# A two-layer transformer stack on one core: 72 of the second attention's exponentials computed on VectorE, and idle matmuls placed on open sums

## The chip, the cores and the metric

The kernel runs on one core of a Trainium2 chip. The engines that matter are TensorE (PE, with its weight loads shown as PEld), ScalarE (ACT), VectorE (DVE) and the DMA queue of SyncE (SP). The metric is the device time of one launch in microseconds (us); of several timed runs the median counts. A profiled execution gives the trace; its time stands beside its span below.

## The reference, cut to what matters

Four blocks run one after the other on `x` (2048 rows of 1024, bf16): linear attention A, softmax attention B, then A and B again with the same weights. "First" and "second attention" below are the two runs of B. There are 32 heads of 32 columns.

```python
def _B_ref(x, wqkv, wo):
    qkv = (x @ wqkv).reshape(B, S, 3, H, Dh).transpose(2, 0, 3, 1, 4)
    q, k, v = qkv[0], qkv[1], qkv[2]
    scores = einsum("bhqd,bhkd->bhqk", q, k) * (Dh ** -0.5)
    p = softmax(scores, axis=-1)
    o = einsum("bhqk,bhkd->bhqd", p, v)
    return o.transpose(0, 2, 1, 3).reshape(B, S, D) @ wo

x = x + A(layernorm(x));  x = x + B(layernorm(x))
x = x + A(layernorm(x));  x = x + B(layernorm(x))
```

One attention makes 32 x 2048 x 2048 exponentials.

## The kernel before, in words

**Order.** Nothing is issued directly. Every piece of work is an `Op` with an engine, a planned duration, dependencies, buffers and a priority. `Sched.run` plays the program with these planned durations and writes down the order in which each engine would start its pieces; the instructions are then emitted in that order, and each engine works its own list strictly in order. Buffers come from an arena in SBUF and from the eight PSUM banks, with a quota for each class (`QUOTA`).

**Attention** (`attention`, L893 on). The work falls into 32 turns, one for each pair of a chunk of 512 queries (`qc`) and a group of four heads (`g`): first chunks 0 and 1 for all groups (turns 0 to 15), then chunk 2 (16 to 23) and chunk 3 (24 to 31). A turn has 64 units. A unit is the 128 x 512 scores of one head: 128 keys against 512 queries. Units are taken three at a time (`WIDE`): three score matmuls (L922), which lie on different 32-row strips of the PE array, fill three PSUM banks, and one ACTIVATE of 128 x 1536 (L928) writes their exponentials to SBUF as bf16. Two such sets of three banks alternate (banks 0 to 5). Per attention that is 682 ACTIVATEs of 1536 columns and one of 1024.

The exponentials are then multiplied with the values and with ones (L956), four matmuls on four 32-column strips at a time, and summed in bank 6 over the whole of half a turn. VectorE copies the sum out of bank 6 (L968); two DMAs on SP move the denominators, VectorE takes four reciprocals (L979) and multiplies (L983).

**Filler.** Bank 7 serves everything else that runs during an attention: the projections of keys (`b_k`), queries (`b_q`, `q_away`) and values (`b_v`), and the output projection, all through L401 as four column strips and each copied out by VectorE (L814, L822, L838). The queries are multiplied by 1/sqrt(32) on that way.

**Idle matmuls.** If PE finds nothing to start in the planned time while scores are live, and has worked less than `KEEP` = 75% of the last `SPELL` = 3.4 planned us, `Sched.run` puts one matmul with no use (`idle`, onesD times x) into bank 7, provided bank 7 is free and no filler holds it. In the trace these are the `xT,onesD` matmuls of L401.

**Pointer operand.** Of all ACTIVATEs before the change, those at L477 alone (the logarithm in the layer norm) take their bias from a 128 x 1 tile, `eps`; the others, L928 too, have scale and bias as constants in the instruction.

Of the kernel before, what the change touches and what calls it, by code (L numbers as in the profile page):

```python
# [2 lines left out]

# [8 lines left out]
AX = mybir.AxisListType  # L12
BF16 = mybir.dt.bfloat16
F32 = mybir.dt.float32

EPS_LN = 1e-5
EPS_DEN = 1e-6
DH = 32
# [12 lines left out]


class Op:
    __slots__ = ("eng", "dur", "lat", "fn", "bufs", "prio", "mode", "ndep", "out", "t", "start", "seq")

    def __init__(self, eng, dur, lat, fn, bufs, prio, mode, seq):
        self.eng, self.dur, self.lat, self.fn, self.bufs = eng, dur, lat, fn, bufs
        self.prio, self.mode, self.seq = prio, mode, seq
        self.ndep, self.out, self.t, self.start = 0, [], 0.0, None


LAT = {"PE": 0.25, "ACT": 0.2, "DVE": 0.1, "POOL": 0.2, "SP": 2.0, "AQ": 2.0}
# [3 lines left out]
class Sched:  # L46
    def __init__(self, sbuf_bytes, quota):
        self.ops = []
        self.quota = quota
        self.live = {}  # L50
        self.free = [(0, sbuf_bytes)]
        self.bank_used = [False] * 8
        self.peak = 0
        self.total = sbuf_bytes
        self.queue = {}
        self.idle = None
# [86 lines left out]
    def run(self):  # L143
# [16 lines left out]
        todo = sorted(o.prio for o in self.ops)  # L160
        front = 0
        recent = []
        started = {}
        for o in self.ops:
            if o.ndep == 0:
# [2 lines left out]
        while left:  # L168
            moved = False
            for e in engines:  # L170
                if busy[e] > t + 1e-9 or not ready[e]:
                    continue
                skipped = []
                pick = None
                while ready[e] and len(skipped) < 60:
                    item = heapq.heappop(ready[e])
                    if item[0] <= todo[front] + WINDOW and self._alloc(item[2].bufs):
                        pick = item[2]
                        break
                    skipped.append(item)  # L180
                for s in skipped:
                    heapq.heappush(ready[e], s)
                if pick is None and e == "PE" and self.idle is not None and self.live.get("S", 0):

                    recent = [r for r in recent if r[1] > t - SPELL]
                    worked = sum(r[1] - max(r[0], t - SPELL) for r in recent)
                    if worked < KEEP * SPELL and not self.live.get("fil", 0) and not self.bank_used[7]:
                        pick = Op("PE", MM, LAT["PE"], self.idle, (Buf("ps", 0, "idle", [(7,)]),), 0.0, "c", 0)
                        pick.bufs[0].left = 1
                        self.queue["idle"] = [list(pick.bufs), 0]  # L190
                        assert self._alloc(pick.bufs)
                        left += 1
                if pick is None:
                    continue
                if e == "PE":
                    recent.append((t, t + pick.dur))
                d = pick.dur
                if pick.mode is not None:
                    if mode[e] is not None and mode[e] != pick.mode:
                        d += SWITCH  # L200
                    mode[e] = pick.mode
                pick.start = t
                if pick.fn is not self.idle:
# [12 lines left out]
            if moved:  # L216
                continue
            if not events:
                stuck = [(o.prio, o.eng, [(b.cls, b.at) for b in o.bufs]) for e in engines for _, _, o in ready[e]][:8]
                raise AssertionError(f"nothing can start at {t:.1f}: {left} left, {stuck}, live {self.live}")  # L220
            t = events[0][0]
            while events and events[0][0] <= t + 1e-9:
                _, _, o, own = heapq.heappop(events)
                if not own:
                    for b in o.bufs:
                        b.left -= 1
                        if b.left == 0:
# [17 lines left out]
QUOTA = {"pk": 3, "pv": 2, "kv": 1, "ln": 2, "mm": 2, "cmp": 2, "bc": 4, "num": 1, "wt": 4, "fil": 2,  # L245
         "e": 6, "vp": 6, "e1": 4, "vp1": 4, "E": 5, "q2": 3, "kt": 3, "w2": 8, "w2o": 3, "oT": 26, "T": 4, "den": 2,
         "lnt": 6, "lnw": 2, "lnw1": 1, "eq": 8, "ns": 4, "cw": 6, "hl": 6, "oc": 2, "slab": 7, "slabk": 3, "fin": 4,
         "rs": 8, "pkf": 1}
SPELL = 3.4
KEEP = 0.75  # L250


def act_us(n):
# [11 lines left out]
def kernel(  # L265
# [16 lines left out]
    NC = S // C512  # L282
    TB = C512 // P
    assert D == 1024 and S % C512 == 0
    inv_sqrt_dh = float(DH**-0.5)

    A_w = A_wqkv.rearrange("(po pi) f -> pi po f", pi=P)
    B_w = B_wqkv.rearrange("(po pi) f -> pi po f", pi=P)
# [12 lines left out]

    onesD = const.tile([P, P], BF16, tag="onesD")
    ones_bf = const.tile([P, DH], BF16, tag="ones")
    J_bf = const.tile([P, P], BF16, tag="J")
    ident = const.tile([P, P], BF16, tag="ident")
    rep = const.tile([P, DH], BF16, tag="rep")
# [3 lines left out]
    hl = const.tile([P, 1], F32, tag="hl")  # L310
    eps = const.tile([P, 1], F32, tag="eps")
    zz = const.tile([P, 16], F32, tag="zz")

    nc.vector.memset(onesD[:], 1.0 / D)
    nc.vector.memset(ones_bf[:], 1.0)
    nc.vector.memset(J_bf[:], 0.0)
    nc.vector.memset(eps[:], EPS_LN)
    for j in range(4):
        nc.vector.memset(J_bf[32 * j:32 * (j + 1), 32 * j:32 * (j + 1)], 1.0)
    make_identity(nc, ident[:])  # L320
# [495 lines left out]
    def b_q(g, c, prio, w, banks):  # L816
        wb, ww, wd = w
        xb, xv, fin = xnB[c]
        pb, pv = ps("fil", banks)
        m = mmg2(pb, pv, lambda po: ww()[:, po, :], lambda po: xv()[:, po, :], fin, wd, [xb, wb], prio)  # L820
        q_b, q_v = sb("q2", 2, C512)
        cp = op("DVE", dve_us(512), lambda: nc.vector.tensor_scalar(  # L822
            out=q_v()[:, 0, :], in0=pv(), scalar1=inv_sqrt_dh, scalar2=None, op0=ALU.mult), [m], [pb, q_b], prio)
        return q_b, q_v, q_swap(q_b, q_v, cp, prio)

    def q_swap(q_b, q_v, cp, prio):
# [4 lines left out]
    def q_away(g, c, prio, w, banks):  # L831

        wb, ww, wd = w
        xb, xv, fin = xnB[c]
        pb, pv = ps("fil", banks)
        m = mmg2(pb, pv, lambda po: ww()[:, po, :], lambda po: xv()[:, po, :], fin, wd, [xb, wb], prio)
        a_b, a_v = sb("kt", C512)
        cp = op("DVE", dve_us(512), lambda: nc.vector.tensor_scalar(  # L838
            out=a_v(), in0=pv(), scalar1=inv_sqrt_dh, scalar2=None, op0=ALU.mult), [m], [pb, a_b], prio)
# [53 lines left out]
    def attention(base, kT, vT, q_of, gate):  # L893
# [6 lines left out]
        first = {}  # L900
        ex_of, e_of = {}, {}
        n = 0
        i = 0
        while i < len(units):
# [14 lines left out]
            def sfn(grp=grp, s_v=s_v):  # L919
# [6 lines left out]
                        start=True, stop=True, tile_position=(32 * j, 0))  # L926
            so = op("PE", 0.24, sfn, deps + (gate if n == 0 else []), [s_b, *bufs], prio - 2, mode="r")
            ex = op("ACT", act_us(w * C512), lambda s_v=s_v, e_v=e_v, w=w: nc.scalar.activation(  # L928
                out=e_v()[:, 0:w * C512], in_=s_v(), func=ACT.Exp), [so], [s_b, e_b], prio - 3)
            for x, u in enumerate(grp):  # L930
                ex_of[u] = ex
                e_of[u] = (e_b, e_v, x)
# [3 lines left out]
        if True:  # L936
            for qc, g in turns:
                T = []
                for pp in range(2):
                    a_b, a_v = ps("acc", [(6,)])  # L940
                    last = None
                    for d in range(8):
                        prio = base + 10 * pos[(qc, g)] + 5 * pp + 0.5 * d
                        for u in range(2):
# [18 lines left out]
                            if e_of[us[1]][0] is not ebs[0]:  # L963
                                ebs.append(e_of[us[1]][0])
                            last = op("PE", 0.225, fn, flat([last, ex_of[us[0]], ex_of[us[1]], v_done[kc % 4]]),
                                      [a_b, v_b, *ebs], prio - 1, mode="c")
                    t_b, t_v = sb("T", C512, dt=F32)
                    cp = op("DVE", dve_us(512), lambda t_v=t_v, a_v=a_v: nc.vector.tensor_copy(out=t_v(), in_=a_v()),  # L968
                            [last], [a_b, t_b], prio - 4)
# [45 lines left out]
    for layer in range(2):  # L1015
# [63 lines left out]
        for g in range(G):  # L1079
            pr = at + 10 * pos[(0, g)]  # L1080
            w = slab("w2", pr - 11, B_w[:, :, g * P:(g + 1) * P], P) if g else wq0
            for qc in range(NC):
# [6 lines left out]
        oTs, last_s = attention(at, kT, vT, q_of, gate)  # L1089
# [27 lines left out]
    def idle():  # L1117
        mm(psum[:, 7 * C512:8 * C512], onesD[:], xT[:, 0, 0:C512], True, True, True)
    sch.idle = idle

    for o in sch.run():
        o.fn()
# [30 lines left out]
```

## Time and profile before

| | us |
|---|---|
| timed runs: lowest, median, highest | 2578.86, 2579.17, 2579.24 |
| the profiled execution: time, span | 2574.77, 2573.0 |
| ACT busy over the span | 2178.7 (85%) |
| L928 exponentials, 1366 instructions, busy | 1845.4 |
| PE busy, with idle matmuls | 2344.9 (91%) |
| DVE busy | 1132.4 (44%) |
| first attention's exponentials | about 375 to 1351 |
| second attention's exponentials | about 1608 to 2546 |

A busy PE is not a PE at its peak: matmul ends are modelled, and idle matmuls count as busy. The share of an engine over the whole span mixes the attentions with the stages between them, so the stages are read one by one. A time given for an instruction is its own duration; neighbours on ACT overlap, so the step from one to the next is shorter.

### The profile page before, as it was taken

To read this page: it belongs to the slowest core of one execution; us is meant where nothing else is said; L and a number is where in the kernel's file an instruction comes from. 1 tells how busy PE (TensorE), PEld (TensorE's weight loads), DVE (VectorE), ACT (ScalarE), POOL (GpSimd) and SP (SyncE) were. 2 spreads that over 40 slices of the span, in tenths; PEclk is the share of its full clock that TensorE was granted. 3 is DMA by queue.
4 is the path that set the end of the run, shared out by engine and by line. 5 is a ranking of instruction groups with operands and counts; after the bars stand their busy time and mean duration, and the time that the engine had idled before them with its cause. 6 is when DMAs were issued, how large, how long until landed. Compare 5 with 4: busy or idle time off the path is not lost.

```text
span 2573.0 us, 59988 instructions
## 1 busy us (share of the span) xinstructions
PE 2344.9 (91%) x26631; PEld 890.6 (35%) x26700; DVE 1132.4 (44%) x1614; ACT 2178.7 (85%) x1919; POOL 25.7 (1%) x72
## 2 busy tenths in 40 slices
PE   7999999999988989899888999999998898889887
PEld 4443433333323333333333344333332233333333
DVE  6997652333322346655526665333432233213222
ACT  6335558999999999999992554899999999999996
POOL 0000000000000000000000000000000000000000
PEclk9999999999989999999999999999999999999999
DMA  9110101112120212223123001111121011001000
GB/s 214 42 34 2 30 15 44 42 34 51 32 73 26 59 44 67 83 75 110 48 67 105 1 7 35 47 36 36 40 63 30 22 38 34 20 18 40 18 16 23
DMA packets 185315, 117.19 MB, mean 46 GB/s; under 512 B 103392, under 2 KB 175072, under 8 KB 184288
## 3 DMA queue, kind: packets, MB, share of 16 engines
q1 hardware_dynamic: 184000, 111.26, 16.3%
q8 instruction: 208, 3.41, 0.6%
q10 hardware_dynamic: 1056, 2.10, 0.3%
q14 instruction: 51, 0.42, 0.1%
HBM read 61.93 MB, written 15.73 MB: 30 GB/s over the span
## 4 chain that ended last, share of the span: by engine, by line
ACT 31%; PE 12%; issue 6%; DVE 2%; DMA 0%; SPq 0%; ACTq 0%; another core or an unknown queue 0%; DVEq 0%
ACT arena L928 30%; PE psum L397 7%; PE psum L401 1%; PE psum L956 1%; PE psum L922 1%; DMA arena<-arena 0%; PE psum L755 0%; DVE arena L979 0%; DVE arena L591 0%; DVE arena L600 0%; SPq L806 0%; DVE arena L777 0%; DVE arena L489 0%; DVE arena L983 0%; PE psum L700 0%
## 5 line engine op out<-in xcount | busy, mean ns | idle before, releaser
L928 ACT ACTIVATE arena<-psum 128x1536 bf16<-128x1536 f32 (+1 forms) x1366 | 1845.4, 1562 | 47.4 <-PE psum L922 43.4
L956 PE MATMUL psum<-arena 128*32 128x512 bf16 x4096 | 713.6, 390 | 12.7 <-ACT arena L928 10.9
L956 PE MATMUL psum<-arena,ones_bf 128*32 128x512 bf16 x4096 | 714.9, 390 | 0.0
L922 PE MATMUL psum<-arena 32*128 32x512 bf16 x4096 | 536.9, 386 | 138.2 <-ACT arena L928 130.9
L401 PE MATMUL psum<-arena 128*32 128x512 bf16 x7872 | 552.4, 382 | 11.9 <-DVE arena L838 2.3
L397 PE MATMUL psum<-arena 128*128 128x512 bf16 x2067 | 488.8, 383 | 35.4 <-DVE arena L983 12.7
L922 PEld LDWEIGHTS <-arena 32*128 32x128 bf16 x4096 | 183.9, 91 | 646.5 <-issue 635.2
L968 DVE COPY arena<-psum 128x512 f32<-128x512 f32 x128 | 88.3, 690 | 491.5 <-PE psum L956 484.6
L397 PEld LDWEIGHTS <-arena 128*128 128x128 bf16 x2128 | 202.7, 98 | 287.3 <-issue 51.5
L401 PEld LDWEIGHTS <-arena 128*32 128x32 bf16 x7872 | 203.3, 96 | 209.6 <-issue 67.0
L956 PEld LDWEIGHTS <-arena 128*32 128x32 bf16 x4096 | 167.9, 94 | 283.4 <-issue 259.6
L979 DVE RECIPROCAL arena<-arena 128x128 f32<-128x128 f32 x256 | 219.4, 912 | 92.0 <-DMA arena<-arena 91.4
L814 DVE CAST arena<-psum 128x512 bf16<-128x512 f32 x116 | 80.2, 691 | 300.9 <-PE psum L401 286.2
L401 PE MATMUL psum<-xT,onesD 128*32 128x512 bf16 x2476 | 205.2, 382 | 0.6 <-DVE xT L865 0.3
L956 PEld LDWEIGHTS <-ones_bf 128*32 128x32 bf16 x4096 | 162.0, 94 | 70.9 <-issue 60.2
L587 ACT ACTIVATE arena<-psum 128x512 bf16<-128x512 f32 x80 | 42.7, 600 | 86.4 <-PE psum L397 54.9
L717 ACT ACTIVATE arena<-psum 128x512 bf16<-128x512 f32 x128 | 69.9, 598 | 42.3 <-PE psum L397 31.0
L600 DVE TENSOR_TENSOR arena<-psum,arena 128x1024 bf16<-128x1024 f32 x64 | 78.3, 1224 | 42.7 <-PE psum L401 38.9
L983 DVE TENSOR_TENSOR arena<-arena 64x512 bf16<-64x512 f32 x128 | 87.8, 686 | 14.1 <-PE psum L956 9.7
L485 DVE TENSOR_TENSOR arena<-xT,arena 128x1024 f32<-128x1024 bf16 x64 | 77.9, 1218 | 36.2 <-ACT arena L474 35.8
L452 ACT ACTIVATE arena<-xT 128x2048 bf16<-128x2048 bf16 x26 | 49.3, 1917 | 47.2 <-DVE xT L865 21.8
L759 ACT COPY arena<-psum 128x512 f32<-128x512 f32 x64 | 37.3, 582 | 60.0 <-PE psum L755 59.8
(82 smaller groups left out, 1068.8 us busy)
## 6 DMA issues: line engine op xcount, KB each, us to landing
arena<-arena SPq DMA_DIRECT2D x128, 128.0 KB, 2.3
arena<-in_A_wqkv_dram SPq DMA_DIRECT2D x10, 1024.0 KB, 5.4
arena<-in_B_wqkv_dram SPq DMA_DIRECT2D x32, 256.0 KB, 3.2
arena<-arena SPq DMA_DIRECT2D x256, 32.0 KB, 1.9
arena<-in_B_wo_dram SPq DMA_DIRECT2D x32, 256.0 KB, 3.1
arena<-wd_k SPq DMA_DIRECT2D x8, 1024.0 KB, 6.1
arena<-in_A_wo_dram SPq DMA_DIRECT2D x4, 1024.0 KB, 6.0
arena<-in_B_wqkv_dram SPq DMA_DIRECT2D x4, 1024.0 KB, 5.5
```

Of the source, the lines that this page charges most:

```text
L397: nc.tensor.matmul(out_, lhsT=lhsT, rhs=rhs, start=start, stop=stop, skip_group_check=True)
L401: nc.tensor.matmul(out_[ks, :], lhsT=lhsT[:, ks], rhs=rhs, start=start, stop=stop, tile_position=(0, 32 * k), skip_group_check=True)
L485: s1 = op("DVE", dve_us(1024), lambda pr=pr, w_v=w_v: nc.vector.tensor_tensor(out=w_v(), in0=xT[:, pr, csl(c)], in1=m_v().unsqueeze(1).to_ ...
L600: ml = op("DVE", dve_us(1024), lambda vpv=vpv, wv_=wv_, sv=sv: nc.vector.tensor_tensor(out=wv_()[:, :, :, 0:DH], in0=vpv().rearrange("p (h ...
L717: ex = [op("ACT", act_us(512), lambda s=s, pv=pv, ev=ev: nc.scalar.activation(out=ev()[:, s, :], in_=pv(), func=ACT.Exp, scale=(1.0, -1.0) ...
L814: return op("DVE", dve_us(512), lambda: nc.vector.tensor_copy(out=dst(), in_=src()), [dep], bufs, prio)
L922: nc.tensor.matmul(out=s_v()[:, x * C512:(x + 1) * C512], lhsT=kT[g][1]()[r, pp, d * P:(d + 1) * P], rhs=q_of[(qc, g)][1]()[r, (pp + j // ...
L928: ex = op("ACT", act_us(w * C512), lambda s_v=s_v, e_v=e_v, w=w: nc.scalar.activation(out=e_v()[:, 0:w * C512], in_=s_v(), func=ACT.Exp), ...
L956: nc.tensor.matmul(out=a_v()[col:col + 32, :], lhsT=v_v()[:, kc % 4, o:o + DH] if what == 0 else ones_bf[:], rhs=ev()[:, x * C512:(x + 1) ...
L968: cp = op("DVE", dve_us(512), lambda t_v=t_v, a_v=a_v: nc.vector.tensor_copy(out=t_v(), in_=a_v()), [last], [a_b, t_b], prio - 4)
L979: rc = [op("DVE", 128 * 8 / 960 + 0.12, lambda b=b, d_v=d_v, r_v=r_v: nc.vector.reciprocal(out=r_v()[:, b * P:(b + 1) * P], in_=d_v()[:, b ...
L983: s = [op("DVE", dve_us(512), lambda a=a, b=b, k=k, o_v=o_v, r_v=r_v, T=T: nc.vector.tensor_tensor(out=o_v()[a, :], in0=T[k][1]()[a, :], i ...
```

## The change

Line numbers in this section are those of the changed kernel. For 36 pairs of units in the second attention alone (turns 8 to 15: one pair each; turns 16 to 29: two pairs each) the scores go one unit at a time through bank 7 (class `xs`, one at a time), and VectorE makes the exponential: the score is `log2(e^s)/4`; it is rounded to a multiple of 1/4 by adding a large number (L936), the remainder is taken (L939), the rounded part becomes the bits of a power of two (L942), and a polynomial of degree four in the remainder is multiplied with it (three at L947, one at L950). The pair's units are the fourth head (`j` = 3) at key blocks `d` = 2 and 3.

The polynomial's leading coefficient is one, so its result is 0.408 times the exponential. For the same factor everywhere, all ACTIVATE exponentials of both attentions get `scale=4*ln 2` (a constant) and `bias=lns`, a 128 x 1 tile with ln 0.408; the queries are divided by 4 ln 2 in `b_q` and `q_away`. The softmax's quotient removes the factor.

`idle_acc` is a second sort of idle matmul: four column strips of zeros times x, added to the open sum in bank 6. It is placed when PE has worked under 75% and bank 7 is taken, if the last PE piece of the sum was not its last one (`accum`).

Per attention the built program has, before and after: first attention 683 and 683 exponential ACTIVATEs, second 683 and 659. Over the whole program the onesD idle matmuls go from 595 groups of four to 161, and 716 groups of four of the new sort are added. The number of DMAs is the same.

```diff
@@ Sched.run @@
                     worked = sum(r[1] - max(r[0], t - SPELL) for r in recent)
-                    if worked < KEEP * SPELL and not self.live.get("fil", 0) and not self.bank_used[7]:
+                    if worked >= KEEP * SPELL:
+                        pass
+                    elif self.bank_used[7]:
+
+                        if accum:
+                            pick = Op("PE", MM, LAT["PE"], self.idle_acc, (), 0.0, "c", 0)
+                            left += 1
+                    elif not self.live.get("fil", 0):
                         pick = Op("PE", MM, LAT["PE"], self.idle, (Buf("ps", 0, "idle", [(7,)]),), 0.0, "c", 0)
...
+                    if pick.accum is not None:
+                        accum = pick.accum
...
+         "xs": 1, "xu": 2, "xg": 2, "xx": 2, "E1": 3}
...
+LEAD = 5.0
+EXTRA = (lambda i: [],
+         lambda i: [(pp, 2) for pp in range(2)] if 16 <= i < 30 else [(i % 2, 2)] if 8 <= i < 16 else [])
...
+    q_scale = float(DH**-0.5 / (4 * math.log(2)))
...
+    zero = const.tile([P, DH], BF16, tag="zero")
+    lns = const.tile([P, 1], F32, tag="lns")
+    nc.vector.memset(zero[:], 0.0)
+    nc.vector.memset(lns[:], math.log(POW2_S))
...
+    def exp_dve(qc, g, pp, d, prio, kT, q_of):
...
+        for k in range(2):
+            s_b, s_v = ps("xs", FIL)
...
+            so = op("PE", MM, sfn, flat([kT[g][2][(d + k) // 2], q_of[(qc, g)][2]]),
+                    [s_b, kT[g][0], q_of[(qc, g)][0]], prio, mode="r")
+            uo = op("DVE", dve_us(512), lambda k=k, s_v=s_v: nc.vector.tensor_scalar(
+                out=u_v()[:, k, :], in0=s_v(), scalar1=-31.5, scalar2=ROUND, op0=ALU.max, op1=ALU.add),
+                [so], [s_b, u_b], prio + 0.01)
+            gs.append(op("DVE", dve_us(512), lambda k=k, s_v=s_v: nc.vector.scalar_tensor_tensor(
+                out=g_v()[:, k, :], in0=u_v()[:, k, :], scalar=ROUND, in1=s_v(), op0=ALU.subtract, op1=ALU.subtract),
+                [uo], [s_b, u_b, g_b], prio + 0.01))
+        wo = op("DVE", 1024 / 1920 + 0.15, lambda: nc.vector.tensor_scalar(
+            out=u_v().bitcast(I32), in0=u_v(), scalar1=ROUND - 31.75, scalar2=float(2**25),
+            op0=ALU.subtract, op1=ALU.mult), gs, [u_b], prio + 0.02)
+        last = gs
+        for i, c in enumerate(POW2_C):
+            last = [op("DVE", dve_us(1024), lambda i=i, c=c: nc.vector.scalar_tensor_tensor(
+                out=x_v(), in0=(x_v() if i else g_v()), scalar=c, in1=g_v(), op0=ALU.add, op1=ALU.mult),
+                last, [g_b, x_b], prio + 0.02)]
+        eo = op("DVE", dve_us(1024), lambda: nc.vector.scalar_tensor_tensor(
+            out=e_v(), in0=x_v(), scalar=POW2_0, in1=u_v(), op0=ALU.add, op1=ALU.mult),
+            [wo, *last], [x_b, u_b, e_b], prio + 0.02)
+        return eo, (e_b, lambda: e_v().rearrange("p a b -> p (a b)"))
@@ attention @@
+        for qc, g in turns:
+            for pp, d in extra(pos[(qc, g)]):
+                eo, (e_b, e_v) = exp_dve(qc, g, pp, d, base + 10 * pos[(qc, g)] + 5 * pp + 0.5 * d - LEAD, kT, q_of)
+                for k in range(2):
+                    ex_of[(qc, g, pp, d + k, 3)] = eo
+                    e_of[(qc, g, pp, d + k, 3)] = (e_b, e_v, k)
+        units = [u for u in units if u not in ex_of]
...
             ex = op("ACT", act_us(w * C512), lambda s_v=s_v, e_v=e_v, w=w: nc.scalar.activation(
-                out=e_v()[:, 0:w * C512], in_=s_v(), func=ACT.Exp), [so], [s_b, e_b], prio - 3)
+                out=e_v()[:, 0:w * C512], in_=s_v(), func=ACT.Exp, scale=4 * math.log(2), bias=lns[:, 0:1]),
+                [so], [s_b, e_b], prio - 3)
...
+                            last.accum = (d, u) != (7, 1)
@@ after the layers @@
+    def idle_acc():
+        for k in range(4):
+            nc.tensor.matmul(psum[32 * k:32 * k + 32, 6 * C512:7 * C512], lhsT=zero[:], rhs=xT[:, 0, 0:C512],
+                             start=False, stop=False, tile_position=(0, 32 * k), skip_group_check=True)
```

More of the change, by code (lines that the diff above doesn't have):

```diff
@@ L1 @@
 import heapq
+import math
 from contextlib import ExitStack
@@ L14 @@
 F32 = mybir.dt.float32
+I32 = mybir.dt.int32
 EPS_LN = 1e-5
@@ L33 @@
 class Op:
-    __slots__ = ("eng", "dur", "lat", "fn", "bufs", "prio", "mode", "ndep", "out", "t", "start", "seq")
+    __slots__ = ("eng", "dur", "lat", "fn", "bufs", "prio", "mode", "ndep", "out", "t", "start", "seq", "accum")
     def __init__(self, eng, dur, lat, fn, bufs, prio, mode, seq):
@@ L38, in __init__ @@
         self.prio, self.mode, self.seq = prio, mode, seq
-        self.ndep, self.out, self.t, self.start = 0, [], 0.0, None
+        self.ndep, self.out, self.t, self.start, self.accum = 0, [], 0.0, None, None
 LAT = {"PE": 0.25, "ACT": 0.2, "DVE": 0.1, "POOL": 0.2, "SP": 2.0, "AQ": 2.0}
@@ L55, in __init__ @@
         self.queue = {}
-        self.idle = None
+        self.idle = self.idle_acc = None
     def op(self, eng, dur, fn, deps=(), bufs=(), prio=0.0, lat=None, mode=None):
@@ L162, in run @@
         recent = []
+        accum = False
         started = {}
@@ L202, in run @@
                 pick.start = t
-                if pick.fn is not self.idle:
+                if pick.fn not in (self.idle, self.idle_acc):
                     started[pick.prio] = started.get(pick.prio, 0) + 1
@@ L247 @@
          "lnt": 6, "lnw": 2, "lnw1": 1, "eq": 8, "ns": 4, "cw": 6, "hl": 6, "oc": 2, "slab": 7, "slabk": 3, "fin": 4,
-         "rs": 8, "pkf": 1}
+         "rs": 8, "pkf": 1,
+         "xs": 1, "xu": 2, "xg": 2, "xx": 2, "E1": 3}
 SPELL = 3.4
 KEEP = 0.75
+ROUND = 1.5 * 2**21
+POW2_0, *_C = (0.4081719430184994, -1.1316523471792392, 1.5689974432587064, -1.4607435989358193)
+POW2_C = _C[::-1]
+POW2_S = 0.40817224447665074
+LEAD = 5.0
+EXTRA = (lambda i: [],
+         lambda i: [(pp, 2) for pp in range(2)] if 16 <= i < 30 else [(i % 2, 2)] if 8 <= i < 16 else [])
 def act_us(n):
@@ L284 @@
     assert D == 1024 and S % C512 == 0
-    inv_sqrt_dh = float(DH**-0.5)
+    q_scale = float(DH**-0.5 / (4 * math.log(2)))
     A_w = A_wqkv.rearrange("(po pi) f -> pi po f", pi=P)
@@ L822, in b_q @@
         cp = op("DVE", dve_us(512), lambda: nc.vector.tensor_scalar(
-            out=q_v()[:, 0, :], in0=pv(), scalar1=inv_sqrt_dh, scalar2=None, op0=ALU.mult), [m], [pb, q_b], prio)
+            out=q_v()[:, 0, :], in0=pv(), scalar1=q_scale, scalar2=None, op0=ALU.mult), [m], [pb, q_b], prio)
         return q_b, q_v, q_swap(q_b, q_v, cp, prio)
@@ L838, in q_away @@
         cp = op("DVE", dve_us(512), lambda: nc.vector.tensor_scalar(
-            out=a_v(), in0=pv(), scalar1=inv_sqrt_dh, scalar2=None, op0=ALU.mult), [m], [pb, a_b], prio)
+            out=a_v(), in0=pv(), scalar1=q_scale, scalar2=None, op0=ALU.mult), [m], [pb, a_b], prio)
         return dma(prio, lambda: nc.sync.dma_start(out=qd_v[:, c - 2, g, :], in_=a_v()), [cp], [a_b], kb=128)
@@ L891, in b_last, with sfn, attention @@
             out=out[0, xs, fc * C512:(fc + 1) * C512], in_=r_v()), [e], [r_b], kb=128)
-    def attention(base, kT, vT, q_of, gate):
+    def exp_dve(qc, g, pp, d, prio, kT, q_of):
+        u_b, u_v = sb("xu", 2, C512, dt=F32)
+        g_b, g_v = sb("xg", 2, C512, dt=F32)
+        x_b, x_v = sb("xx", 2, C512, dt=F32)
+        e_b, e_v = sb("E1", 2, C512)
+        r = slice(96, 128)
+        gs = []
+        for k in range(2):
+            s_b, s_v = ps("xs", FIL)
+            def sfn(k=k, s_v=s_v):
+                nc.tensor.matmul(
+                    out=s_v(), lhsT=kT[g][1]()[r, pp, (d + k) * P:(d + k + 1) * P],
+                    rhs=q_of[(qc, g)][1]()[r, (pp + 1) % 2, :], start=True, stop=True, tile_position=(96, 0))
+            so = op("PE", MM, sfn, flat([kT[g][2][(d + k) // 2], q_of[(qc, g)][2]]),
[18 more added lines that the diff above has]
+        return eo, (e_b, lambda: e_v().rearrange("p a b -> p (a b)"))
+    def attention(base, kT, vT, q_of, gate, extra):
         units = [
@@ L899, in attention @@
         ]
-        first = {}
         ex_of, e_of = {}, {}
+        for qc, g in turns:
[5 more added lines that the diff above has]
+        units = [u for u in units if u not in ex_of]
         n = 0
@@ L1088 @@
                     q_of[(qc, g)] = q_back(g, qc, at + 10 * pos[(qc, g)] - 12, away)
-        oTs, last_s = attention(at, kT, vT, q_of, gate)
+        oTs, last_s = attention(at, kT, vT, q_of, gate, EXTRA[layer])
         if last:
@@ L1119 @@
     sch.idle = idle
+    def idle_acc():
+        for k in range(4):
+            nc.tensor.matmul(psum[32 * k:32 * k + 32, 6 * C512:7 * C512], lhsT=zero[:], rhs=xT[:, 0, 0:C512],
+                             start=False, stop=False, tile_position=(0, 32 * k), skip_group_check=True)
+    sch.idle_acc = idle_acc
     for o in sch.run():
```

## The prediction

> **What bounds the kernel now.** First the page: the busy shares over the span, the slices, the chain of waits, and the costliest group.
>
> ```profile
> PE 2344.9 (91%) x26631; PEld 890.6 (35%) x26700; DVE 1132.4 (44%) x1614; ACT 2178.7 (85%) x1919; POOL 25.7 (1%) x72
> ...
> ACT  6335558999999999999992554899999999999996
> ...
> ACT 31%; PE 12%; issue 6%; DVE 2%; DMA 0%; SPq 0%; ACTq 0%; another core or an unknown queue 0%; DVEq 0%
> ...
> L928 ACT ACTIVATE arena<-psum 128x1536 bf16<-128x1536 f32 (+1 forms) x1366 | 1845.4, 1562 | 47.4 <-PE psum L922 43.4
> ```
>
> PE has the highest share, but the slices show ACT at nine tenths or more in slices 8 to 21 and 27 to 39, most of the two attentions, and ACT leads the chain. Which of them sets the time is read from busy time by stretch (columns: length, then PE, PEld, DVE, ACT busy, PE's granted clock).
>
> ```profile
> 395.00:720.00 325.00, 308.47 (x4283) 107.38 (x4281) 114.21 (x156) 318.70 (x238) 0.00 (x0) 1.00 0.16 39
> 720.00:880.00 160.00, 143.00 (x1736) 46.15 (x1739) 40.78 (x55) 155.16 (x116) 0.00 (x0) 0.91 0.20 52
> ...
> 1625.00:1900.00 275.00, 263.77 (x3688) 92.55 (x3692) 96.44 (x132) 268.88 (x201) 0.00 (x0) 1.00 0.18 46
> 1900.00:2050.00 150.00, 132.41 (x1654) 42.88 (x1643) 41.60 (x56) 147.17 (x110) 0.00 (x0) 0.94 0.11 27
> ...
> 2200.00:2520.00 320.00, 285.46 (x3753) 100.44 (x3752) 73.80 (x97) 319.96 (x239) 0.00 (x0) 1.00 0.08 22
> ```
>
> From 2200 to 2520 ACT is busy for 319.96 of 320 us: the exponentials set the time, one each 1.34 us (320/239). ACT lacks 6.3 us in the first stretch and 6.1 in the third, where PE is 95 and 96% busy, and 4.8 and 2.8 where the clock is 0.91 and 0.94. The two stretches not shown, 880 to 1350 and 2050 to 2200, lack 5.7 and 0.1 us. In all 26 us of the two attentions are not ACT's.
>
> **The change, part by part.**
>
> *Removed: 24 exponentials.* The second attention loses 72 of 2048 units, three to an ACTIVATE. 24 x 1.344 = 32.3 us, of ACT time that is on the path (turns 8 to 29 run from about 1850 to 2490, where ACT is full).
>
> *Added: a bias read from a tile, on all 1342 ACTIVATEs that stay, 683 and 659.* The scale is a constant as before and costs nothing: L479 (scale -0.5) lasts 630 ns, L740 (scale 1) 631, on the same form. For the bias one line has a counterpart, L477 with its `eps`. By line:
>
> ```profile
> L477 ACT ACTIVATE arena<-arena,eps x16: 721/724/943, 23.6 to 1610.3; 128x512 f32<-128x512 f32 x16
> ...
> L740 ACT ACTIVATE arena<-arena x16: 629/631/656, 189.7 to 1577.8; 128x512 f32<-128x512 f32 x16
> ```
>
> Same form, 93 ns longer with the tile. The function is not the reason: logarithm and exponential from PSUM (L771, L717) last 597 and 598 ns. But ACTIVATEs overlap, and an exponential of 1.58 us steps by 1.344, so what counts is whether the 93 ns lengthen the step. The timeline of ACT answers, by ends of neighbours (start, length, line):
>
> ```profile
> 240.69 1.09 ACT L717 ACTIVATE arena<-psum 128x512 bf16<-128x512 f32 x2 [1.50 <-PE psum L397]
> 241.66 0.72 ACT L477 ACTIVATE arena<-arena,eps 128x512 f32<-128x512 f32 x1
> ...
> 250.10 1.08 ACT L717 ACTIVATE arena<-psum 128x512 bf16<-128x512 f32 x2 [0.64 <-PE psum L397]
> 251.07 0.63 ACT L740 ACTIVATE arena<-arena 128x512 f32<-128x512 f32 x1
> ...
> 952.80 2.93 ACT L928 ACTIVATE arena<-psum 128x1536 bf16<-128x1536 f32 x2
> 955.48 0.84 ACT L477 ACTIVATE arena<-arena,eps 128x512 f32<-128x512 f32 x1
> ...
> 1071.09 2.95 ACT L928 ACTIVATE arena<-psum 128x1536 bf16<-128x1536 f32 x2
> 1073.94 1.14 ACT L587 ACTIVATE arena<-arena 128x512 bf16<-128x512 f32 x2
> ```
>
> After L717, the line with the tile ends 0.60 us after its predecessor (241.66+0.72 against 240.69+1.09), L740 without it 0.52. After exponentials, where the next one starts a quarter of a us before the last has ended, L477 ends 0.59 later (956.32 against 955.73), and the two L587 take 1.04 together (1075.08 against 1074.04), 0.52 each. So the overlap does not hide the read: the step grows by 0.07 to 0.09. No row shows a stream in which every member has a tile, nor one that reads the tile while its data come from PSUM; the ends are 0 (the read could run under the predecessor's quarter of a us) and 0.093 (L477's own length). Less than nothing is excluded, since a read is added. I take 0.080, between 0.07 and 0.09. First attention 683 x 0.080 = 54.6 us, second 659 x 0.080 = 52.7.
>
> The Trainium skill, "ScalarE: Activation LUTs", section "What ACT_TABLE_LOAD costs", gives about 93 ns for each such operand, in the length of an instruction. The trace agrees on the length. By the page alone the sum below would end about 17 us higher.
>
> *What a longer step gives back.* Where PE was late, ACT waited; with 6% more time for each exponential PE catches up. Of the 12.4 us in the two crowded stretches I count 10 as gone. The 7.7 us at a lowered clock: there PE had little to do. In the built order, turn 12 of both attentions holds 70 steps of PE work of 0.217 us (score triples, and strips in fours), 15.2 of 28.7 us (64/3 x 1.344); every other turn has 18.2 or more, and those with 18.2, idle matmuls among them, keep the clock at 1.00. With the new idle matmuls no turn of either attention has less than 19.1, turns 12 have 21.3 and 20.4 of some 30, so I count 6 of the 7.7 as gone. Of the rest 1. Together 17; bounds 0 and 26.
>
> *Added on VectorE.* One pair: 2 x 0.69 (L936, like the copy out of PSUM, L968) + 2 x 0.69 (L939, like L475, PSUM and SBUF in, f32 out, 688 ns) + L942 between 0.85 (twice the 0.424 of the SBUF cast L684) and 1.22, taken at 0.85 since it too has one SBUF source + 4 x 1.22 (L947, L950, like L489): 8.5 us, 36 pairs 306. The fullest part, turns 16 to 29, gets 28 pairs, 238 us. DVE had 97.8 us of work from 2069 to 2460 and would have about 336 of the 14 x 20 x 1.424 = 399 us that ACT needs: 84%. I cost it at nothing; the cover is ACT's own time. Each first step (L936) waits for a score matmul, and behind it in DVE's order stands the copy out of bank 6, for which PE's next sum waits, and behind that the scores. These sums start half a turn ahead (`LEAD`), so a late one has some 14 us before its product is due.
>
> *Added on PE.* 72 single score matmuls less 24 triples, (72-24) x 0.217 = 10.4 us over 22 turns of 28 us, and idle matmuls, each at most 0.22 us ahead of a due score. Scores have one exponential's time, 1.34 us, to appear and take 0.39, so nothing shows. Bank 7 is shared with the projections, which the built order moves some turns later (turn 46 has 40 projection matmuls where there were none); a late one costs waits like those of the crowded stretches, up to 1.3 us each. No DMA is added. Two memsets more at the start, under 0.1 us each, before the first data come.
>
> *Sum.* -32.3 + 54.6 + 52.7 - 17 = +58 us. On the profiled execution's own 2574.8 us (span 2573.0) that makes 2633; the median of the runs shown, 2579.2, lies 4.4 higher, so 2637 for a timed run.
>
> **The rivals.**
>
> *1. The tile read hides in a stream (faster).* If the read of the next bias runs under the quarter of a us by which exponentials overlap, the step stays 1.344. Then 32.3 us and the 6 us at a lowered clock go: 2579 - 38 = 2541. For it: the overlap of 0.24 us is longer than 0.093, and sources in PSUM leave SBUF free. Against it: after L928, with just this overlap, L477 still came 0.07 later. It decides below a growth of (32.3+12)/1342 = 0.033 us.
>
> *2. DVE becomes the bound (slower than forecast).* In turns 16 to 29 DVE has 399 - 336 = 63 us to spare, 1.1 us for each of 56 units. If every L936 waits longer than that for its scores, because bank 7 goes back and forth between PE and DVE, copies out of bank 6 come late. At 2 us each: 336 + 112 = 448, 49 us more: 2686. For it: DVE waits up to 14.1 us for L956 now. Against: these waits are idle time that nobody needs.
>
> *3. Zeros do not keep the clock.* If matmuls on zero weights do not count as work, turns 48 to 60 fall to about 16 us of counted work per 28, near turn 12 before. There, 3.2 us held 0.41 us of ACT's waiting at half clock (0.41 each from 757 to 767). If 400 of the 600 us went so, 51 us: 2688. For it: the onesD idle matmuls vanish in these turns. Against: the strips stream the same x columns.
>
> *4. The change buys nothing:* the growth comes out near 0.033, and the time within 0.2% of before. No row lies near this.
>
> **How the numbers follow.** Forecast 0.79; rival 1 0.09; rival 2 0.05; rival 3 0.05; rival 4 0.02. The forecast's own ends: a growth of 0.05 gives 67 - 32 - 17 = +18, 2597; 0.093 with nothing given back 125 - 32 = +93, 2672. The low end of the range stands at 2600; the high end reaches toward rivals 2 and 3, 2680. That leaves out rival 1, rival 4 and half of 2 and 3. A difference of 0.2%, 5 us, is about what a measurement of this kernel tells from none. Slower: forecast, rivals 2 and 3, less the forecast's own tail, 0.88; same 0.02; faster 0.10.
>
> **What would show it.** Right: exponentials with the tile step by 1.41 to 1.44 us in both attentions, the first attention longer by 40 to 60 us although no work was taken from it, the second by 10 to 25, DVE near 80% from turn 16 on without lengthening ACT's waits, the clock at 1.00 throughout both attentions. Wrong: a step of 1.34 (rival 1), or ACT waiting for PE while PE waits for DVE's copy (rival 2), or a clock of 0.5 in the late turns (rival 3).

## The result, and the profile after

| | us |
|---|---|
| before: median of 4 (lowest, highest) | 2579.2 (2578.9, 2579.8) |
| after: median of 4 (lowest, highest) | 2654.3 (2650.8, 2655.4) |
| ratio, 95% interval | 1.0289, 1.0271 to 1.0306 |
| profiled executions, before and after | 2574.8 and 2655.4 (spans 2573.0 and 2653.6) |

The change makes the kernel 75 us slower. The page of the kernel after: busy shares, two engines by slices, the chain by engine, and the group of exponentials.

```profile
PE 2416.5 (91%) x27759; PEld 926.5 (35%) x27828; DVE 1425.1 (54%) x1940; ACT 2262.6 (85%) x1895; POOL 25.9 (1%) x72
...
DVE  6996653333222345655525665333455677677842
ACT  6335559999999999999993564899999999999996
...
ACT 50%; PE 25%; issue 14%; DVE 8%; SPq 1%; DMA 1%; another core or an unknown queue 0%; ACTq 0%; DVEq 0%
...
L996 ACT ACTIVATE arena<-psum,lns 128x1536 bf16<-128x1536 f32 x1342 | 1929.3, 1702 | 42.9 <-PE psum L990 37.9
```

There are 24 exponentials fewer and yet 84 us more of them (1929.3 against 1845.4): one now lasts 1.70 us instead of 1.56. VectorE is busy 293 us longer (1425 against 1132), most of it in the last third. ACT still fills the attentions.

The chain of waits of the kernel after, in a part of the first attention where ACT never waits (start, length, what):

```profile
810.29 2.67 ACT arena L996 x2
816.01 2.81 ACT arena L996 x2
...
838.91 2.82 ACT arena L996 x2
841.77 2.67 ACT arena L996 x2
```

From 838.91 to 841.77 two exponentials take 2.86 us, and four from 810.29 to 816.01 take 5.72: 1.43 each. Over all neighbours the median distance of ends is 1.431 us, against 1.343 before. By stage, from the first start and last end of the exponentials (before, the first attention's begin at 358.1, the second's at 1590.9; the starts in the table of times above, about 375 and 1608, leave out the first two of each; differences are taken before rounding):

| stage | before | after | difference |
|---|---|---|---|
| first attention | 992.7 | 1046.1 | +53.3 |
| between | 240.0 | 239.2 | -0.8 |
| second attention | 955.4 | 982.1 | +26.8 |
| start and tail | 384.9 | 386.1 | +1.3 |

The first attention lost no work to VectorE and grew most. Busy time by stretch of the kernel after (length, PE, PEld, DVE, ACT, POOL busy, PE's granted clock, then the DMA engines' busy share and GB/s):

```profile
395.00:740.00 345.00, 323.38 (x4475) 116.14 (x4471) 114.40 (x156) 339.51 (x237) 0.00 (x0) 1.00 0.15 37
740.00:930.00 190.00, 171.70 (x2327) 61.49 (x2323) 51.95 (x69) 190.00 (x134) 0.00 (x0) 1.00 0.20 53
...
2157.00:2564.00 407.00, 363.75 (x4822) 124.72 (x4819) 306.70 (x362) 401.14 (x281) 0.00 (x0) 0.98 0.10 26
```

Where the clock stood at 0.91 before, ACT is now busy for 190 of 190 us at 1.00. From 2157 to 2564, turns 16 to 29 of the second attention, VectorE is busy 75% of the time and ACT 98.6%. The 5.9 us that ACT lacks there stand where the clock falls to half: 3.9 around 2534.4 to 2544.6, 2.0 after two dips of 3.4 us (at 2189.7 and 2449.1).

### The profile page after: what moved, and what is told of

Its sections match the earlier page's. It is cut to its first block, busy times and chain, and to the rows that moved or that the text cites. A ratio compares the mean times of both kernels' runs of the same rounds, so it can differ in the third digit from the quotient of the medians.

```text
span 2653.6 us, 62693 instructions
## 1 busy us (share of the span) xinstructions
PE 2416.5 (91%) x27759; PEld 926.5 (35%) x27828; DVE 1425.1 (54%) x1940; ACT 2262.6 (85%) x1895; POOL 25.9 (1%) x72
## 4 chain that ended last, share of the span: by engine, by line
ACT 50%; PE 25%; issue 14%; DVE 8%; SPq 1%; DMA 1%; another core or an unknown queue 0%; ACTq 0%; DVEq 0%
ACT arena L996 47%; PE psum L423 14%; PE psum L1025 3%; PE psum L427 3%; PE psum L990 3%; DVE arena L617 1%; SPq L458 1%; DVE arena L947 1%; ACT arena L613 1%; DVE arena L515 1%; PE psum L781 1%; DVE arena L626 1%; DVE arena L511 1%; PE psum L1193 1%; DVE arena L1049 1%
## 5 line engine op out<-in xcount | busy, mean ns | idle before, releaser
L996 ACT ACTIVATE arena<-psum,lns 128x1536 bf16<-128x1536 f32 x1342 | 1929.3, 1702 | 42.9 <-PE psum L990 37.9
L1025 PE MATMUL psum<-arena 128*32 128x512 bf16 x4096 | 710.8, 386 | 20.4 <-ACT arena L996 15.5
L1025 PE MATMUL psum<-arena,ones_bf 128*32 128x512 bf16 x4096 | 712.1, 387 | 0.0
L990 PE MATMUL psum<-arena 32*128 32x512 bf16 x4024 | 523.3, 383 | 146.4 <-ACT arena L996 127.9
L1025 PEld LDWEIGHTS <-arena 128*32 128x32 bf16 x4096 | 167.1, 94 | 274.5 <-issue 249.8
L1049 DVE RECIPROCAL arena<-arena 128x128 f32<-128x128 f32 x256 | 221.1, 915 | 49.1 <-DMA arena<-arena 48.8
L1193 PE MATMUL psum<-xT,zero 128*32 128x512 bf16 x2864 | 229.0, 385 | 0.0
L1025 PEld LDWEIGHTS <-ones_bf 128*32 128x32 bf16 x4096 | 160.0, 94 | 89.6 <-issue 82.3
L947 DVE SCALAR_TENSOR_TENSOR arena<-arena 128x1024 f32<-128x1024 f32 x108 | 132.0, 1222 | 3.6 <-PE psum L1025 1.3
L626 DVE TENSOR_TENSOR arena<-psum,arena 128x1024 bf16<-128x1024 f32 x64 | 78.5, 1226 | 47.1 <-PE psum L427 42.9
L1193 PEld LDWEIGHTS <-zero 128*32 128x32 bf16 x2864 | 74.2, 97 | 68.7 <-issue 17.1
```

The lines of the kernel that those rows point to most:

```text
L626: ml = op("DVE", dve_us(1024), lambda vpv=vpv, wv_=wv_, sv=sv: nc.vector.tensor_tensor(out=wv_()[:, :, :, 0:DH], in0=vpv().rearrange("p (h ...
L947: last = [op("DVE", dve_us(1024), lambda i=i, c=c: nc.vector.scalar_tensor_tensor(out=x_v(), in0=(x_v() if i else g_v()), scalar=c, in1=g_ ...
L990: nc.tensor.matmul(out=s_v()[:, x * C512:(x + 1) * C512], lhsT=kT[g][1]()[r, pp, d * P:(d + 1) * P], rhs=q_of[(qc, g)][1]()[r, (pp + j // ...
L1025: nc.tensor.matmul(out=a_v()[col:col + 32, :], lhsT=v_v()[:, kc % 4, o:o + DH] if what == 0 else ones_bf[:], rhs=ev()[:, x * C512:(x + 1) ...
L1049: rc = [op("DVE", 128 * 8 / 960 + 0.12, lambda b=b, d_v=d_v, r_v=r_v: nc.vector.reciprocal(out=r_v()[:, b * P:(b + 1) * P], in_=d_v()[:, b ...
L1193: nc.tensor.matmul(psum[32 * k:32 * k + 32, 6 * C512:7 * C512], lhsT=zero[:], rhs=xT[:, 0, 0:C512], start=False, stop=False, tile_position ...
```

## The experiments

**e1: the same bias as a constant.** The order of every engine is that of the kernel after.

```diff
-  func=ACT.Exp, scale=4 * math.log(2), bias=lns[:, 0:1])
+  func=ACT.Exp, scale=4 * math.log(2), bias=math.log(POW2_S))
```

> The changed kernel with the same bias, ln 0.408, as a constant in the instruction; the order of every engine is that of the changed kernel. Theory (the tile read lengthens each exponential's step, 1.431 against 1.343 us, and nothing else makes the change slow): the step returns to 1.343, so 1342 x 0.088 = 118 us less than the changed kernel, about 2536 to 2545, faster than the kernel before. Rival (VectorE's exponentials or the shared bank 7 are what slows it): stays above 2579. If VectorE becomes the limit once the step is short, the saving falls short of 118 by up to 40 us, with ACT waiting for PE from turn 16 on.

Measured: 2538.7 us, ratio to the kernel before 0.984 (0.982 to 0.985); 115.6 us under the kernel after. The group of exponentials on its page, where 1929.3 us stood with the tile:

```profile
L996 ACT ACTIVATE arena<-psum 128x1536 bf16<-128x1536 f32 x1342 | 1811.3, 1573 | 43.1 <-PE psum L990 41.9
```

The median step is back at 1.343. So the tile read alone, 115.6/1342 = 0.086 us each, turns a gain of 41 us into a loss of 75. VectorE and bank 7 are no part of the loss.

**e2: the tile alone, in the kernel before.** A tile of zeros is the bias; no other change.

```diff
+  nc.vector.memset(lns[:], 0.0)
-  func=ACT.Exp)
+  func=ACT.Exp, bias=lns[:, 0:1])
```

> The kernel before, with a tile of zeros as the bias of its 1366 exponentials and nothing else. Theory: the step grows by 0.088 us, 120 us, less what ACT's waits give back (7 in the first attention, about 3 in the second): 2579 + 110 = 2690. Rival (the growth comes from the scale of 4 ln 2 or from VectorE's traffic in SBUF): about 2579.

Measured: 2698.0 us, ratio 1.046 (1.044 to 1.048), 118.4 us more, 0.087 for each of 1366. The step shows in its chain of waits:

```profile
829.60 2.76 ACT arena L930 x2
832.45 2.78 ACT arena L930 x2
835.29 2.79 ACT arena L930 x2
```

Two in 2.84 to 2.85 us: 1.43 again, with neither the new scale nor VectorE's traffic, so the rival falls in both its forms. The growth of 0.088 on 1366 would be 120.2 us; of the 10 us that were expected back 1.8 came. ACT still waits 13.9 us for scores (L924) in the first attention, where it waited 14.0 before. The mean clock of this kernel's runs is also lower, 0.978 to 0.982 against 0.979 to 0.985, so some of what the longer step gave back may have gone to the clock. The cleaner pair is e1 and the kernel after, with one order, two steps and the clock at 1.00 in these stretches: ACT lacks 6.5 us in e1 from 395 to 720 and 5.5 in the kernel after from 395 to 740, and 6.0 (1625 to 1840) and 5.3 (1678 to 1960) in the second attention. The longer step gives back 1.7 of 12.5 us.

Why it gives so little back is seen at single waits. ACT before, then after, at the end of a turn of the second attention (start, length, line, idle time before it):

```profile
1644.85 4.16 ACT L928 ACTIVATE arena<-psum 128x1536 bf16<-128x1536 f32 x3
1649.89 1.45 ACT L928 ACTIVATE arena<-psum 128x1536 bf16<-128x1536 f32 x1 [0.88 <-PE psum L922]
```

```profile
1698.54 4.41 ACT L996 ACTIVATE arena<-psum,lns 128x1536 bf16<-128x1536 f32 x3
1703.83 1.54 ACT L996 ACTIVATE arena<-psum,lns 128x1536 bf16<-128x1536 f32 x1 [0.88 <-PE psum L990]
```

And PE of the kernel before at that moment:

```profile
1648.87 0.38 PE L956 MATMUL psum<-arena 128*32 128x512 bf16 x1
...
1649.06 0.38 PE L956 MATMUL psum<-arena 128*32 128x512 bf16 x1
...
1649.39 0.39 PE L922 MATMUL psum<-arena 32*128 32x512 bf16 x4
```

The wait is 0.88 us in both. In PE's order the next scores (L922) stand behind the last products of the turn (L956), and the second pair of these starts at 1649.06, just after the exponential that it multiplies has ended (1644.85 + 4.16 = 1649.01). ACT has finished and its next scores are still to be made. That is a round trip laid down by the order, not a lack of speed, and the slower ACT did not shorten it.

Other waits are of a second kind. ACT before, PE before, and ACT after, at one of them:

```profile
433.34 2.79 ACT L928 ACTIVATE arena<-psum 128x1536 bf16<-128x1536 f32 x2 [1.32 <-PE psum L922]
```

```profile
430.98 1.65 PE L401 MATMUL psum<-arena 128*32 128x512 bf16 x24
```

```profile
435.63 2.97 ACT L996 ACTIVATE arena<-psum,lns 128x1536 bf16<-128x1536 f32 x2 [1.23 <-PE psum L990]
```

Here a block of 24 filler matmuls stands in PE's order between products and the next scores. The longer step takes 0.09 us off the wait, about what it grew by, and no more: the block itself waits for products behind ACT's last exponentials, so PE can't use the longer step to run far ahead. Of the nine waits of e1 from 395 to 720, the two of the first kind are 0.88 and 1.25 us in the kernel after as well; of the other seven two vanish, four shrink by 0.08 to 0.31, and one grows by 0.07.

**e3: the idle matmuls alone.** No VectorE exponentials, no tile, the old scale.

```diff
-  oTs, last_s = attention(at, kT, vT, q_of, gate, EXTRA[layer])
+  oTs, last_s = attention(at, kT, vT, q_of, gate, EXTRA[0])
-  func=ACT.Exp, scale=4 * math.log(2), bias=lns[:, 0:1])
+  func=ACT.Exp)
-  q_scale = float(DH**-0.5 / (4 * math.log(2)))
+  q_scale = float(DH**-0.5)
```

> The kernel before with the new idle matmuls alone: 648 groups of zeros onto bank 6, 436 groups of onesD, no VectorE exponentials, no tile, the old scale. Theory (zeros count as work for the clock): the stretches at half clock in both attentions vanish, ACT loses 7.7 us less of waiting there, of which some 6 return: 2573. Rival (zeros do not count): clock dips as before or more, 2579 or above. Rival (idle matmuls get in the way of scores): above 2579 with the clock at 1.00.

Measured: 2567.9 us, ratio 0.995 (0.994 to 0.997). The two stretches that had 0.91 and 0.94 of the clock before:

```profile
720.00:880.00 160.00, 150.62 (x2085) 52.24 (x2081) 42.46 (x57) 160.00 (x120) 0.00 (x0) 1.00 0.21 55
1900.00:2050.00 150.00, 140.90 (x1948) 48.59 (x1948) 41.70 (x56) 150.00 (x113) 0.00 (x0) 1.00 0.10 26
```

The clock is 1.00 and ACT full in both; the 4.8 and 2.8 us that ACT lacked there are back. The spans of the profiled executions differ by 6.4 us (2573.0, 2566.6), near the expected 6; the medians by 11.8 (2579.6, 2567.9). The rest goes with the clock too: the timed runs of the kernel before go from 2578.3 us at a mean clock of 0.985 to 2588.2 at 0.979, all above its profiled execution (2574.8 at 0.986), while those of e3 all show 0.995 and lie within 1.7 us. So the profiled execution showed less of the loss than a usual run has. (Counted as in the section on the change, the trace has 410 idle onesD groups here and 226 in e4, where the expectations say 436 and 252.)

**e4: e1 without the new idle matmuls.**

```diff
                     elif self.bank_used[7]:
-                        if accum:
+                        if False:
```

> As e1, without the idle matmuls on bank 6 (252 groups of onesD stay). Theory (zeros count): turns 8 to 29 of the second attention hold about 16 us of PE work in 27, near turn 12 of the kernel before, so the clock falls to half there again and again, and the time is 10 to 50 us above e1. Rival (zeros do not count or the clock does not matter): equal to e1 within 3 us.

Measured: 2573.2 us, ratio 0.997 (0.996 to 0.998), 34.6 above e1. Busy time in turns 16 to 29, first e1, then e4:

```profile
2070.00:2455.00 385.00, 357.17 (x4925) 122.49 (x4925) 309.60 (x367) 382.78 (x286) 0.00 (x0) 1.00 0.11 29
```

```profile
2070.00:2490.00 420.00, 362.62 (x3947) 105.28 (x3946) 316.71 (x374) 399.03 (x292) 0.00 (x0) 0.83 0.10 27
```

Without the zeros the clock is 0.83 and ACT lacks 21 us instead of 2; of the 34.6 us, 31.6 lie in the second attention (953.4 against 921.8). Zeros count as work for the clock, and without them the whole change, with the constant bias, brings 6.4 us of the 41.

**e5: units of the first attention too.** One pair in each of its turns 8 to 29, on top of e1.

```diff
-EXTRA = (lambda i: [],
+EXTRA = (lambda i: [(i % 2, 2)] if 8 <= i < 30 else [],
```

> As e1 (constant bias), and the first attention gives VectorE one pair of units in each of turns 8 to 29: 44 units, 14.7 exponentials fewer, 19.7 us of ACT. Theory (as long as VectorE has room, each exponential taken away is worth its step): DVE is busy for 27% there between 720 and 880 and 52% between 880 and 1350, and gets some 8.35 us for each turn of 28, at most 82%; 2538.7 - 19.7, with 2 to 3 us lost as in e1: about 2521. Rival (the layer norms and key products that run on VectorE inside the first attention come late, and the stage between the attentions grows): 2535 or more, with the first attention shorter and the next stage longer.

Measured: 2558.1 us, ratio 0.991 (0.990 to 0.993), 19 us above e1: the rival's size, but not its place. The stage between the attentions is hardly longer (240.2 us against 239.9 in e1); the first attention itself grows from 989.6 to 1007.1 us. ACT's waits between 880 and 1355:

```profile
ACT arena L996 <- PE psum L990: 18.2, 26, 2.9
ACT arena L996 <- PE psum L1025: 13.0, 3, 6.3
ACT arena L996 <- DVE arena L950: 7.9, 1, 7.9
```

Three waits of 7.9, 6.3 and 6.3 us make up half of this, though VectorE is busy for only 69% there (154.87 of 220 us, then 172.04 of 255). The longest ends with VectorE's exponential: L950 ends at 976.99, ACT starts at 977.08. The first steps (L936) of that pair's two units stand 15.3 us apart, at 954.68 and 970.00, with sums and products of the linear attention's keys (L610, L617, L626) and the reciprocals of denominators (L1049) between them. Room by the average is not room at each place in a fixed order. What held the other two waits was not followed to its end.

**e6: three pairs in turns 16 to 29.**

```diff
-         lambda i: [(pp, 2) for pp in range(2)] if 16 <= i < 30 else [(i % 2, 2)] if 8 <= i < 16 else [])
+         lambda i: [(0, 2), (1, 2), (i % 2, 4)] if 16 <= i < 30 else [(i % 2, 2)] if 8 <= i < 16 else [])
```

> As e1, with three pairs instead of two in turns 16 to 29 of the second attention: 28 units, 9.3 exponentials fewer, 12.5 us of ACT. Theory (the cover of VectorE's work ends at ACT's time for a turn): a turn holds 7.0 + 3 x 8.35 = 32 us of VectorE's work against 58/3 x 1.343 = 26.0 of ACT's, so VectorE sets the turn at 32 or more, 14 turns x 5 to 6 us above e1's 26.9: 2538.7 + 75 = 2614. If cover were left: 2526.

Measured: 2607.3 us, ratio 1.010 (1.009 to 1.012), 69 above e1. Busy time there, and ACT's longest waits:

```profile
2070.00:2500.00 430.00, 390.20 (x5508) 143.71 (x5505) 395.95 (x466) 353.37 (x261) 0.00 (x0) 1.00 0.09 25
```

```profile
ACT arena L996 <- PE psum L1025: 52.3, 15, 6.3
ACT arena L996 <- PE psum L990: 10.8, 14, 1.7
ACT arena L996 <- DVE arena L950: 7.7, 3, 6.2
```

VectorE is busy for 396 of 430 us, ACT for 353: here VectorE sets the time, 31.7 us for a turn where 32 were forecast. ACT waits for products (L1025), which wait for VectorE's last step (L950). At one of these places L950 ends at 2184.33, the products start at 2184.38, and ACT, idle for 5.60 us, at 2184.88; PE worked off filler and idle matmuls meanwhile, so that its own wait shows as 1.34. That VectorE can become the bound, as in the second rival, is true beyond two pairs a turn.

**e7 and e8: smaller additions.** e7 is e1 with one pair in turns 8 to 15 of the first attention; e8 adds one in turns 4 to 7 of the second.

```diff
-EXTRA = (lambda i: [],
+EXTRA = (lambda i: [(i % 2, 2)] if 8 <= i < 16 else [],
```

and in e8 besides

```diff
-         lambda i: [(pp, 2) for pp in range(2)] if 16 <= i < 30 else [(i % 2, 2)] if 8 <= i < 16 else [])
+         lambda i: [(pp, 2) for pp in range(2)] if 16 <= i < 30 else [(i % 2, 2)] if 4 <= i < 16 else [])
```

> As e1, and the first attention gives VectorE one pair in turns 8 to 15 alone, before layer norms and key products come to VectorE: 16 units, 5.3 exponentials fewer, 7.2 us of ACT. Theory (what e5 lost was lost where this other work stands; before it VectorE was at 63% and ACT never waited): 2538.7 - 7 = 2532. Rival (units in the first attention cost more than they bring in every turn): 2539 or more.

> As e7, with one pair also in turns 4 to 7 of the second attention, where the projections crowd bank 7: 8 units more, 2.7 exponentials, 3.6 us of ACT. Theory (VectorE has room there, 35% busy, and bank 7 can give it): 2528. Rival (the shared bank is the limit there, and late keys and queries make ACT wait): 2532 or more, with new waits of ACT for scores before turn 12.

Measured: 2537.8 us (ratio 0.983, 0.982 to 0.985) and 2540.6 (0.985, 0.983 to 0.986). The first attention of e7 is 7.4 us shorter than e1's (982.2, 989.6), where 7.2 were expected, and the second, whose list of units is the same, 6.2 longer (928.0, 921.8). Most of that is one place, in the waits of e7 from 1864 to 1880:

```profile
ACT arena L996 <- DMA qd<-arena: 4.5, 1, 4.5
```

At 1867.0 ACT runs dry until 1871.5, though PE made its next scores at 1867.21 (0.39 us). It waits for a move of queries out of the arena (`qd<-arena`, L866), issued at 1862.90 and landed at 1871.4. The exponential does not read these queries, so what it waits for must be the place of its output buffer in the arena (read from the waits and the code, not tested). In e1 the same move is nearly as slow, issued at 1869.55 and landed at 1877.2, and no exponential waits for it. From the second attention on, the lists of PE, ACT, VectorE and SP agree line by line in e1 and e7: moving units in one attention left the other's order as it was, and must have changed which buffers share a place. This was the slowest of five runs (2538.6; the fastest 2534.6). In e8 ACT waits 17.6 us from 1620 to the start of turn 12 at 1964, where e7 waits 11.9 to 1960, so its rival holds.

## Why the prediction was right, and by how much its terms were off

The direction, the mechanism of the loss and the range (2600 to 2680) held; the point, 2637, is 17 us low. By its own terms, with the medians of e1 and e3 as steps (2579.6 to 2567.9 to 2538.7 to 2654.3):

| term | forecast | measured |
|---|---|---|
| 24 exponentials fewer | -32.3 | -29.2 (e1 against e3) |
| tile read on 1342, by the growth of the step | +107.3 (0.080 each) | +118.1 (0.088 each) |
| given back where PE was late, and the rest | -11 | -2.5 (118.1 less the 115.6 of e1) |
| given back by the clock | -6 | -11.8 (e3) |
| sum | +58 | +74.6 |

Of its signs, the step of 1.41 to 1.44 (1.431) and the first attention longer by 40 to 60 us (53.3) came true. The second attention, 26.8 us longer, lies just outside 10 to 25; VectorE is at 75%, not near 80; and the clock was not at 1.00 throughout: in the second attention it stood at half three times, 17 us in all.

*The tile read.* This is the term that was most under-sized. The two rows were read from ends printed to 0.01 us. In the trace's nanoseconds the step after L717 is 607 with the tile and 516 without, 91 more; after runs of exponentials it is 588 to 595 (L477) against some 506 to 520 (L587), about 77 more. Rounding took 11 of the 91 ns, and 10 ns on 1342 instructions are 13 us. In a stream where every instruction has the tile the step grows by 0.088, from 1.343 to 1.431; the time by 0.086 for each, as waits elsewhere take up a little. The Trainium skill's 93 ns ("ScalarE: Activation LUTs", "What ACT_TABLE_LOAD costs") is a figure for the length of one instruction; as a price in a stream it is 5 to 7 ns high here. The first rival, that the quarter of a us of overlap hides the read, is refuted by e1 and e2.

*What is given back.* This term failed in its kind. Ten of the 17 us were to come from the crowded stretches, because PE would catch up with a slower ACT. They hardly came: from 395 to 740 ACT still lacks 5.5 us where it lacked 6.3. The single waits show why. PE's 95% had been read as a lack of speed; but the waits are set by what stands before the scores in PE's order, and each gives back nothing (round trips) or at most 0.3 us (the others). The part from the clock was forecast at 6 us from one profiled execution, and e3 gives 11.8 in the medians (6.4 in the profiled executions). The 4.4 us that were added to come from the profiled execution to a timed run belong to the same loss at the lowered clock, which the change removes. That the two errors nearly cancel, 14.3 us given back against 17, is luck.

*Units and VectorE.* The added work was sized well. By form, two of its costliest steps and L942, of the kernel after:

```profile
L947 DVE SCALAR_TENSOR_TENSOR arena<-arena 128x1024 f32<-128x1024 f32 x108 | 132.0, 1222 | 3.6 <-PE psum L1025 1.3
L936 DVE TENSOR_SCALAR arena<-psum 128x512 f32<-128x512 f32 x72 | 49.5, 688 | 84.5 <-PE psum L931 79.3 <-PE psum L1025 2.6 <-ACT arena L996 2.5
...
L942 DVE TENSOR_SCALAR arena<-arena 128x1024 int32<-128x1024 f32 x36 | 25.0, 693 | 1.2
```

Only L942 was guessed too high, 0.85 us against 0.69, below the lower end that was given for it. The sum of the lines' busy times, 300 us, stands beside the forecast's 306. VectorE waits 79 us in 50 waits for the single scores, 1.6 us each, and 52.7 us of these lie in turns 16 to 29; it has them to spare, as it is busy for 306.7 of 407 us there. That the units bring 29.2 and not 32.3 us is for the most part waiting: in the second attention ACT waits for PE 8.3 us in e1 and 6.0 in e3. Of e1's waits 2.0 us stand from 2422 to 2432, at the start of turn 29: a round trip of 1.09 us, and then the clock at half for 3.4 us (2426.2 to 2429.6). In the kernel after the clock is at half for 10.2 us at the same turn, again behind a wait of 1.09.

*The rivals.* The third is refuted: zeros keep the clock (e3, e4), if not at every place. The second did not occur with two pairs, at either step: e1 leaves ACT 2 us of idle time in 385, and the 5.9 us in the kernel after lie at the three dips of the clock, during which PE was busy all the time. It does with three (e6).

The version that beats both kernels is e1: 2538.7 us, 1.6% under the kernel before, by writing the bias as a constant; e7, at 2537.8, can't be told from it.

## What to carry to other kernels

Before an operand of an instruction that runs a thousand times becomes a tile, look for a line that has one already, and compare the distance of ends with a twin that has none, in nanoseconds if the price is to be multiplied by a thousand: a bias equal on all partitions belongs in the instruction. Before a longer step is credited with closing waits, see what the late matmul stands behind: a round trip in a fixed order stays, and one behind a block of filler gives back a few tenths of a us at most. Work moved to an engine with room on average is paid only as far as that engine's work fits into each turn, and only while the buffers around it stay where they do no harm.

## What the runs showed of the hardware

Matmuls on zero weights hold the PE clock as others do (0.83 without them, 1.00 with them, in the same turns). The clock fell though PE never stood still for long: in turn 12 of the first attention before, with work for 15.2 of 28.7 us and no idle time of PE over 0.62 us, it went to half (752.6 to 769.7), and from 2016 to 2551, in turns with 18.2 us or more, it did not. That is no sharp line: the kernel after, with no turn under 19.1 us, still had three dips in the second attention. A conversion from f32 to int32 on VectorE, 128 x 1024 in SBUF from one tile, with a subtraction and a product by constants, takes 0.69 us (L942), where a sum with a constant and a product of two f32 tiles of that size take 1.22 (L947). A bias tile lengthens the step of a stream of 128 x 1536 exponentials from PSUM by 0.088 us, the same constant in the instruction by nothing (1.343 us before and in e1).
